# First token pair by plain products, begun among the attention tiles; the weights' further parts made later

## The chip, the cores and the metric

The kernel runs on one core of one Trainium2 chip. The metric is the time of one execution on the device in microseconds (us), the median over several runs. The engines are named as in the profile: PE is TensorE (matmuls and transposes; PEld its weight loads), DVE is VectorE, ACT is ScalarE, POOL is GpSimd and SP is SyncE, whose queue issues all DMAs of this kernel.

## The reference

Three stages follow one another. The first is chunked attention with four batches, eight heads, 768 positions and a head size of 64: each chunk of 32 queries sees 8 memory positions and a window of 56 neighbours. Its result, put together over the heads, is `x` with 3072 tokens of 512 features. The other two are feed-forward layers:

```
h = x @ w_in                        # 512 -> 2048
x = (h * tanh(softplus(h))) @ w_out # 2048 -> 512
xn = x / sqrt(mean(x*x) + 1e-6) * rms_g
g, val = xn @ w_gate, xn @ w_val    # 512 -> 1536 each
out = (silu(g) * val) @ w_out2      # 1536 -> 512
```

The weights come in 64-bit floating point, everything else in 32 bits.

## The kernel before

**Numbers.** The kernel brings each 64-bit weight tile to 32 bits itself (`cv_all`): a raw tile of 128 x 512 takes two activations on ACT (L168, L171) and three operations on DVE (L173, L174, L180). Every factor of a dense product is then split into a high and a low part (`split`: a cast on ACT, L138, and a subtraction on DVE, L139), and a product is three matmuls: high with high, high with low, low with high (`product`, L525 to L527).

**Fewer products.** A product of two 2 x 2 block matrices is done in seven block products instead of eight (`group`, in the order `ORDER`). It needs sums of blocks on both sides. On the weights' side, `cv_all` makes them after converting both tiles of a pair, and a *slot* holds seven split parts (`W_AT` gives each product's place). On the tokens' side `sum_pieces` (called through `t_pieces`) makes seven split tiles `T` for two token blocks of 384. On the way out, `group` adds up the seven results on ACT, DVE and POOL.

**Tokens and stages.** 3072 tokens are eight blocks, four pairs. Attention runs in tiles of 128 tokens, six to a pair, each in five steps a to e, which `att_list` interleaves over neighbouring tiles. The first six tiles run alone, with the first conversions between their pieces (`CV_START`). Then pair 0 goes through the first dense layer, eight groups (`group1`) with eight weight slots, while the tiles of pair 1 and the other conversions are spread over its 56 steps: `slots` returns the function `between`, which is called after every product, and which also issues stores of slots (`keep_w`), and at the end the sums and splits of the next pair (`tail_of`). Pairs 1 and 2 go alike, without conversions, but with slots reloaded (five buffers for eight slots); pair 3 has no attention beside it. Results go to memory as `g_d` through four buffers `g`.

**Afterwards** comes the second product of the first layer with the norm (`out1`, `rms_pieces`; L608 to L610), then the gated layer (`group2`), then the last product (`group3`, with `h_pieces` for sums and splits; L721 to L723).

**Order.** The tile framework orders each engine's instructions by a planner's times, and waits are put in from the data. `pin` holds an instruction behind all that was written before it for the same engine. SP issues DMAs in its own order too.

Of the kernel before, what the change touches and what calls it, by code (L numbers as in the profile page):

```python
# [24 lines left out]
W_AT = {1: 0, 2: 1, 4: 2, 3: 3, 5: 4, 6: 5, 7: 6}  # L25


@with_exitstack
def tile_kernel(
# [15 lines left out]
    nc = tc.nc  # L45
# [36 lines left out]
    cp = ctx.enter_context(tc.tile_pool(name="cp", bufs=6))  # L82
    psp = ctx.enter_context(tc.tile_pool(name="psp", bufs=1, space=bass.MemoryType.PSUM))
# [57 lines left out]
    jobs, raws, n_load = [], [], [0]  # L141
# [16 lines left out]
    def cv_all():  # L158

        done = 0  # L160
        for kind, key, parts, u, keep, store in jobs:
            tiles, slot = [], None
            for n in range(len(parts)):
                cv_prefetch(done)
                raw = raws.pop(0)
                a = cap.tile([128, 512], I32, tag="ca", name="ca")
                lr = cvp.tile([128, 512], I32, tag="lr", name="lr")
# [3 lines left out]
                nc.scalar.activation(lr, raw[:, :, 0].bitcast(U32), ACTF.Copy, scale=2.0 ** -29)  # L171
                yield
                nc.vector.tensor_scalar(a, a, 3, None, op0=ALU.logical_shift_left)  # L173
# [6 lines left out]
                nc.vector.tensor_tensor(a, a, lr, op=ALU.add)  # L180
# [11 lines left out]
            if kind == "rows":  # L192
                continue
# [10 lines left out]
            def part(i, src):  # L204
                cnt = src.shape[-1] // 256
                src = src.rearrange("p (a f) -> p a f", f=256)
                split(src, w[:, i:i + cnt, 0, :], w[:, i:i + cnt, 1, :])
# [6 lines left out]
            nc.vector.tensor_tensor(s2, s1, a11, op=ALU.subtract)  # L214
# [11 lines left out]
            yield  # L226

# [257 lines left out]
    def sum_pieces(j, b11, b21, b12, b22, new, dram, tab):  # L485
# [11 lines left out]
        def sums():  # L497
# [5 lines left out]
            nc.gpsimd.tensor_tensor(temp[4], temp[2], b21, op=ALU.subtract)  # L503
            nc.gpsimd.tensor_tensor(b12, b22, b12, op=ALU.subtract)
# [13 lines left out]
    def product(p, w, t, bank_, first):  # L518
        ws = w[:, W_AT[p]].rearrange("p l (k f) -> p l k f", k=2)
# [41 lines left out]

    def run(parts, between):
# [17 lines left out]
    def group1_parts(j, i):  # L580
# [3 lines left out]
        mul = lambda p, bank_, first: product(p, wtab["i", i], ts[p], bank_, first)  # L584
# [7 lines left out]
    def group2(j, f):  # L592
# [4 lines left out]
        mul = lambda p, bank_, first: product(p, wtab["gv", f], ts[p], bank_, first)  # L597
# [59 lines left out]
    def rms_pieces(m, n, new):  # L657
# [3 lines left out]
        sq = [cp.tile([128, N], F32, tag="c", name="sq") for _ in range(2)]  # L661
# [79 lines left out]
    CV_START = 22  # L741
# [3 lines left out]
    for i, u in zip(range(F1 // 2), W_SLOT):  # L745
        add_pair(("i", i), w_in, 2 * i, w_in, 2 * i + 1, u, True, False)
# [15 lines left out]

    first = att_list(0)
    for n, piece in enumerate(first):
# [64 lines left out]
    bt = slots((att_list(2), 56), (0, 0), tail_of(2),  # L829
               {n: keep_w(i, half) for i, ns in ((7, (1, 4)), (6, (8, 11)), (5, (15, 18)))  # L830
# [184 lines left out]
```

## Time and profile before

| | |
|---|---|
| median of 3 runs | 1231.05 us (1230.18 to 1231.24) |
| the profiled execution | 1233.01 us, its span 1231.2 us |
| granted clock of PE, mean | 0.976 of full speed |
| busy in the span | PE 95%, DVE 69%, ACT 50%, POOL 25% |
| DMA | 287.48 MB, mean 233 GB/s |

The span runs from the first to the last instruction of the program; the profiled execution's own time has 1.8 us more. All stretches below are in microseconds from the span's start. Busy time of PE counts each matmul from its start to its modelled end, and consecutive ones overlap.

### The profile page before, as it was taken

How to read it: one execution, taken by the hardware profiler on the slowest of the kernel's cores; microseconds unless marked ns; L12 is line 12 of the kernel's file. 1: busy time of each engine (PE TensorE's matmuls, PEld its weight loads, DVE VectorE, ACT ScalarE, POOL GpSimd, SP SyncE). 2: the span in 40 equal slices, each digit the busy share in tenths (PEclk: the TensorE clock that was granted, in tenths of full speed). 3: DMA queues.
4: the chain of work that ended last, by engine and by line, in shares of the span. 5: the costliest groups of instructions: out<-in, count | busy, mean ns of one | idle time of the engine just before them, and what ended most of it. 6: DMA issues, size and time to landing. Idle time of an engine off the chain costs nothing.

```text
span 1231.2 us, 24871 instructions
## 1 busy us (share of the span) xinstructions
PE 1171.6 (95%) x9896; PEld 1126.5 (91%) x9896; DVE 847.3 (69%) x1314; ACT 620.2 (50%) x1050; POOL 311.8 (25%) x251
## 2 busy tenths in 40 slices
PE   6689889999999999999999899999999999999998
PEld 4468869889999999999999899999999999999998
DVE  4598874374486876867676487766667655998883
ACT  3565543243354876677856454444444433444442
POOL 2032230030143321312111222111122121544441
PEclk8689999899999999999999999999999999999999
DMA  9689869879367874757559589969476759745540
GB/s 185 156 232 263 229 195 309 235 201 266 124 259 287 286 251 143 288 170 281 188 171 390 236 296 388 363 247 356 166 285 259 286 205 339 200 140 143 146 138 35
DMA packets 214003, 287.48 MB, mean 233 GB/s; under 512 B 103552, under 2 KB 177280, under 8 KB 209664
## 3 DMA queue, kind: packets, MB, share of 16 engines
q1 hardware_dynamic: 213888, 285.91, 70.4%
q8 instruction: 77, 1.26, 0.4%
q14 instruction: 38, 0.31, 0.1%
HBM read 180.49 MB, written 105.38 MB: 232 GB/s over the span
## 4 chain that ended last, share of the span: by engine, by line
PE 62%; DMA 8%; DVE 7%; ACT 4%; issue 2%; POOL 2%; SPq 0%; DVEq 0%; ACTq 0%; POOLq 0%
PE bk L525 10%; PE bk L526 9%; PE bk L527 9%; PE bk L721 4%; PE bk L722 4%; PE bk L723 4%; DMA T<-nt_scratch 4%; PE bk L609 2%; PE bk L610 2%; PE bk L608 2%; DMA g<-g_scratch 2%; DVE T L139 2%; PE bkp L610 1%; PE bkp L609 1%; PE bkp L608 1%
## 5 line engine op out<-in xcount | busy, mean ns | idle before, releaser
L525 PE MATMUL bk<-T,w 128*128 128x384 f32 x976 | 339.9, 350 | 13.3 <-DMA T<-nt_scratch 3.9
L526 PE MATMUL bk<-T,w 128*128 128x384 f32 x976 | 331.6, 340 | 1.9 <-DVE T L139 1.9
L527 PE MATMUL bk<-T,w 128*128 128x384 f32 x976 | 328.8, 339 | 1.7 <-DVE w L139 1.6
L525 PEld LDWEIGHTS bk<-T,w 128*128 128x128 f32 x976 | 185.8, 191 | 23.9 <-DMA T<-nt_scratch 5.3
L526 PEld LDWEIGHTS bk<-T,w 128*128 128x128 f32 x976 | 185.8, 190 | 3.5 <-DVE T L139 2.9
L527 PEld LDWEIGHTS bk<-T,w 128*128 128x128 f32 x976 | 185.3, 190 | 2.5 <-DVE w L139 2.5
L608 PE MATMUL bk<-T,w 128*128 128x384 f32 x384 | 128.9, 339 | 1.1 <-DVE s L552 1.1
L609 PE MATMUL bk<-T,w 128*128 128x384 f32 x384 | 129.8, 338 | 0.0
L610 PE MATMUL bk<-T,w 128*128 128x384 f32 x384 | 129.0, 336 | 0.0
L721 PE MATMUL bk<-w,T 128*128 128x256 f32 x396 | 111.6, 282 | 0.0
L723 PE MATMUL bk<-w,T 128*128 128x256 f32 x396 | 111.5, 282 | 0.0
L722 PE MATMUL bk<-w,T 128*128 128x256 f32 x396 | 111.3, 281 | 0.0
L552 DVE TENSOR_TENSOR s<-bk,s 128x384 f32<-128x384 f32 (+1 forms) x92 | 49.3, 536 | 89.2 <-PE bk L527 79.7
L556 POOL TENSOR_TENSOR v<-s,z 128x384 f32<-128x384 f32 x48 | 51.1, 1066 | 186.4 <-DVE s L552 103.2
L139 DVE TENSOR_TENSOR T<-w,T 128x768 fp32r<-128x768 f32 x60 | 77.4, 1301 | 11.4 <-ACT T L138 11.4
L722 PEld LDWEIGHTS bk<-w,T 128*128 128x128 f32 x396 | 75.4, 190 | 0.0
L556 POOL TENSOR_TENSOR g<-s,z 128x384 f32<-128x384 f32 x32 | 34.4, 1075 | 161.6 <-DVE s L552 85.2
L721 PEld LDWEIGHTS bk<-w,T 128*128 128x128 f32 x396 | 75.1, 190 | 0.0
L723 PEld LDWEIGHTS bk<-w,T 128*128 128x128 f32 x396 | 75.1, 190 | 0.0
L536 ACT COPY s<-bk 128x384 f32<-128x384 f32 (+1 forms) x92 | 42.6, 463 | 63.0 <-PE bk L527 52.1
L608 PEld LDWEIGHTS bk<-T,w 128*128 128x128 f32 x384 | 72.2, 188 | 1.9 <-ACT w L138 1.4
L609 PEld LDWEIGHTS bk<-T,w 128*128 128x128 f32 x384 | 72.3, 188 | 1.1 <-DVE T L139 0.3
(152 smaller groups left out, 2509.3 us busy)
## 6 DMA issues: line engine op xcount, KB each, us to landing
T<-nt_scratch SPq DMA_DIRECT2D x49, 768.0 KB
g_scratch<-g SPq DMA_DIRECT2D x64, 384.0 KB
g<-g_scratch SPq DMA_DIRECT2D x64, 384.0 KB
h_scratch<-s SPq DMA_DIRECT2D x48, 384.0 KB
w<-h_scratch SPq DMA_DIRECT2D x24, 768.0 KB
w<-wi SPq DMA_DIRECT2D x9, 1792.0 KB
nt_scratch<-T SPq DMA_DIRECT2D x21, 768.0 KB
raw<-in_moe_w_out_dram SPq DMA_DIRECT2D x28, 512.0 KB
```

What stands on the lines that cost most here:

```text
L139: (eng or nc.vector).tensor_tensor(lo, src, hi.bitcast(F32), op=ALU.subtract)
L525: nc.tensor.matmul(ps, whi, xh, start=first and kk == 0, stop=False, **more)
L526: nc.tensor.matmul(ps, whi, xl, start=False, stop=False, **more)
L527: nc.tensor.matmul(ps, wlo, xh, start=False, stop=kk == 1, **more)
L552: nc.vector.tensor_tensor(u3, y, s1, op=ALU.add)
L556: nc.gpsimd.tensor_tensor(c22, u3, z5, op=ALU.add)
L608: nc.tensor.matmul(ps, ahi, bhi, start=start, stop=False)
L609: nc.tensor.matmul(ps, ahi, blo, start=False, stop=False)
L610: nc.tensor.matmul(ps, alo, bhi, start=False, stop=stop)
L721: nc.tensor.matmul(ps, t[:, 0, f], w[:, 0], start=first and f == 0, stop=False, **more)
L722: nc.tensor.matmul(ps, t[:, 0, f], w[:, 1], start=False, stop=False, **more)
L723: nc.tensor.matmul(ps, t[:, 1, f], w[:, 0], start=False, stop=f == HG - 1, **more)
```

## The change

Pair 0 no longer goes through seven-product groups. A new `unit(b, i)` multiplies token block `b` with weight pair `i` by plain products, and results leave through ACT alone. The eight conversions of `w_in` fill only four parts of a slot (`add_plain`); the other three and the changed part 2 are made later by `finish` from the slot itself, so the parts have another order (`W_IN`). Three units of block 0 are made ready when its last attention tile is done; seven of their twelve products are put between attention pieces (`HEADS`), the rest follows the attention. Conversions are held in program order (`in_start`, whose switch `start` stays on to the end), and three slots instead of two are due before the dense part begins. The two sums of `sum_pieces` on POOL go to DVE, for every caller of it. The norm's `sq` tiles get two buffers of their own (`sqp`) instead of two of the six of `cp`.

```diff
+W_IN = {1: 0, 2: 1, 3: 2, 4: 3, 5: 4, 6: 5, 7: 6}
+    sqp = ctx.enter_context(tc.tile_pool(name="sqp", bufs=2))
-    def split(src, hi, lo, eng=None):
-        nc.scalar.copy(hi, src)
-        (eng or nc.vector).tensor_tensor(lo, src, hi.bitcast(F32), op=ALU.subtract)
+    def split(src, hi, lo, eng=None, keep=lambda ins: ins):
+        keep(nc.scalar.copy(hi, src))
+        keep((eng or nc.vector).tensor_tensor(lo, src, hi.bitcast(F32), op=ALU.subtract))
+    jobs, raws, n_load, start = [], [], [0], [True]
+
+    def in_start(ins):
+        return pin(ins) if start[0] else ins
...
+    def add_plain(key, arr, f0, f1, u):
+        jobs.append(("plain", key, [(arr, "col", f0), (arr, "col", f1)], u, True, False))
...
-                nc.scalar.activation(lr, raw[:, :, 0].bitcast(U32), ACTF.Copy, scale=2.0 ** -29)
+                in_start(nc.scalar.activation(
+                    lr, raw[:, :, 0].bitcast(U32), ACTF.Copy, scale=2.0 ** -29
+                ))
...
+                if kind == "plain":
+                    split(a.rearrange("p (a f) -> p a f", a=2), w[:, 2 * n:2 * n + 2, 0, :],
+                          w[:, 2 * n:2 * n + 2, 1, :], keep=in_start)
+                    if n == 1:
+                        wtab[key], wslot[key] = w, slot
+                    yield
+                    continue
...
+    def finish(key):
+        w = wtab[key]
+        aa = [cap.tile([128, 512], F32, tag="ca", name="ca") for n in range(2)]
+        for n, a in enumerate(aa):
+            hi, lo = (w[:, 2 * n:2 * n + 2, l, :].bitcast(F32) for l in range(2))
+            nc.vector.tensor_tensor(a.rearrange("p (a f) -> p a f", a=2), hi, lo, op=ALU.add)
+        a0, a1 = aa
+        a11, a12, a21, a22 = a0[:, 0:256], a0[:, 256:512], a1[:, 0:256], a1[:, 256:512]
+        sm = cvp.tile([128, 4, 256], F32, tag="sm", name="sm")
+        s4, s1, s2, s3 = (sm[:, i, :] for i in range(4))
+        nc.gpsimd.tensor_tensor(s1, a21, a22, op=ALU.add)
+        nc.gpsimd.tensor_tensor(s3, a11, a21, op=ALU.subtract)
+        nc.vector.tensor_tensor(s2, s1, a11, op=ALU.subtract)
+        nc.vector.tensor_tensor(s4, a12, s2, op=ALU.subtract)
+        yield
+        split(s4, w[:, 2, 0, :], w[:, 2, 1, :])
+        yield
+        split(sm[:, 1:4, :], w[:, 4:7, 0, :], w[:, 4:7, 1, :])
+        yield
...
-            nc.gpsimd.tensor_tensor(temp[4], temp[2], b21, op=ALU.subtract)
-            nc.gpsimd.tensor_tensor(b12, b22, b12, op=ALU.subtract)
+            nc.vector.tensor_tensor(temp[4], temp[2], b21, op=ALU.subtract)
+            nc.vector.tensor_tensor(b12, b22, b12, op=ALU.subtract)
...
+    def x_split(b, half):
+        t = t_new()
+        split(xb[b][:, 2 * half:2 * half + 2, :], t[:, 0], t[:, 1])
+        xtab[b, half] = t
+
+    def unit(b, i):
+        need(("i", i))
+        w = wtab["i", i]
+        g = gp.tile([128, 2, N], F32, tag="g", name="g")
+        for e in range(2):
+            ps = bk[(2 * n_unit[0] + e) % 4]
+            for half in range(2):
+                product(2 * e + half, w, xtab[b, half], ps, half == 0)
+                if half:
+                    nc.scalar.copy(g[:, e, :], ps[:, 0:N])
+                    if e:
+                        store_later(
+                            g_d[0, 2 * i:2 * i + 2, :, b, :].rearrange("f p n -> p f n"), g
+                        )
+                yield
+        n_unit[0] += 1
...
-        sq = [cp.tile([128, N], F32, tag="c", name="sq") for _ in range(2)]
+        sq = [sqp.tile([128, N], F32, tag="q", name="sq") for _ in range(2)]
...
-    CV_START = 22
+    CV_START = 24
-    for i, u in zip(range(F1 // 2), W_SLOT):
-        add_pair(("i", i), w_in, 2 * i, w_in, 2 * i + 1, u, True, False)
+    for i in (0, 1, 2, 3, 4, 5, 7, 6):
+        add_plain(("i", i), w_in, 2 * i, 2 * i + 1, W_SLOT[i])
...
+    NHEAD = 3
+    HEADS = (2, 3, 4, 5, 6, 7, 8)
+    heads, at_head = None, 10 ** 6
...
+        if piece[0] == (att_e, NSUB - 1):
+            for half in range(2):
+                x_split(0, half)
+            heads, at_head = [unit(0, i) for i in range(NHEAD)], n
+        elif n - at_head in HEADS:
+            if next(heads[0], "end") == "end":
+                heads.pop(0)
+                next(heads[0])
-    early, rest = t_pieces(0, xb.pop(0), xb.pop(1), t_new, None, ttab_x)
-    for fn in early + rest:
-        fn()
-        flush()
+    for half in range(2):
+        x_split(1, half)
+    for part in heads:
+        run([part], flush)
...
-    CV_I = 88
-    bt = slots((att_list(1), 56), (0, 98), tail_of(1),
-               {n: keep_w(i, half) for i, ns in ((0, (2, 6)), (1, (9, 13)), (2, (17, 22)))
-                for half, n in enumerate(ns)}, CV_I)
-    for i in up:
-        group1(0, i, bt)
+    CV_I = 64
+    units = [(1, i) for i in range(NHEAD)]
+    units += [(b, i) for i in (2, 3, 4, 5, 7, 6) if i >= NHEAD for b in range(2)]
+    at = {u: 4 * n + 4 for n, u in enumerate(units)}
+    more = {}
+    for i in range(3):
+        finish_at(more, i, at[1, i] + 1)
+        for half in range(2):
+            then(more, at[1, i] + 4 + 3 * half, keep_w(i, half))
+    finish_at(more, 7, at[1, 7] + 1)
+    bt = slots((att_list(1), 4 * len(units)), (0, 73), tail_of(1), calls(more), CV_I)
+    for b, i in units:
+        run([unit(b, i)], bt)
+    more = {}
+    for i, ns in ((7, (3, 5)), (6, (9, 12)), (5, (16, 19))):
+        for half, n in enumerate(ns):
+            then(more, n, keep_w(i, half))
+    for n, i in enumerate((6, 5, 4, 3)):
+        finish_at(more, i, 7 * n + 1)
+    bt = slots((att_list(2), 56), (0, 0), tail_of(2), calls(more))
```

The counts of conversion steps in the later stages are lowered to match (eight steps a slot instead of eleven); nothing else changes there.

## Rows read from the trace of the kernel before

**Rows 1.** The page's totals: busy us, share of the span, instructions.

```profile
PE 1171.6 (95%) x9896; PEld 1126.5 (91%) x9896; DVE 847.3 (69%) x1314; ACT 620.2 (50%) x1050; POOL 311.8 (25%) x251
```

**Rows 2.** Windows: length, busy us (instructions) by engine, granted clock, DMA share, GB/s.

```profile
0.00:74.00 74.00, 46.05 (x961) 34.10 (x962) 42.56 (x84) 35.79 (x61) 17.80 (x25) 0.75 0.82 172
74.00:171.60 97.60, 87.81 (x1196) 77.89 (x1197) 83.55 (x156) 56.05 (x106) 26.29 (x25) 0.96 0.92 255
171.60:260.00 88.40, 85.67 (x1133) 78.44 (x1132) 43.22 (x82) 32.09 (x58) 15.28 (x14) 0.96 0.78 231
260.00:343.40 83.40, 82.79 (x1194) 75.86 (x1194) 45.91 (x85) 33.76 (x60) 14.68 (x11) 1.00 0.63 191
...
1047.00:1231.00 184.00, 179.77 (x1505) 179.56 (x1503) 144.83 (x157) 76.49 (x119) 74.16 (x36) 1.00 0.47 134
```

**Rows 3.** Timeline of PE: start, duration, instruction; two at full, two at half clock.

```profile
98.45 0.33 PE L527 MATMUL bk<-T,w 128*128 128x384 f32 x1
98.62 0.33 PE L525 MATMUL bk<-T,w 128*128 128x384 f32 x1
...
74.64 0.52 PE L525 MATMUL bk<-T,w 128*128 128x384 f32 x1
74.96 0.52 PE L526 MATMUL bk<-T,w 128*128 128x384 f32 x1
```

**Rows 4.** The chain that ended last, two pieces of attention in pair 1.

```profile
188.61 0.79 PE bkp L423 x53
...
190.66 0.44 PE bk L406 x4
```

**Rows 5.** Groups of PE by line, 74 to 171.6 us: count, busy, mean ns, idle before.

```profile
L526 PE MATMUL bk<-T,w 128*128 128x384 f32 x110 | 38.6, 351 | 1.3 <-DVE T L139 1.3
```

**Rows 6.** Timeline around the end of the first six attention tiles.

```profile
64.21 0.59 ACT L456 COPY xb<-bk 128x512 f32<-128x512 f32 x1
...
70.72 2.25 POOL L503 TENSOR_TENSOR t<-t,xb 128x768 f32<-128x768 f32 x1
...
73.70 0.95 DVE L139 TENSOR_TENSOR T<-xb,T 128x768 fp32r<-128x768 f32 x1
...
73.84 0.69 PE L526 MATMUL bk<-T,w 128*128 128x384 f32 x1 [1.30 <-DVE T L139]
```

**Rows 7.** Waits of PE, 74 to 171.6 us: total, times, longest.

```profile
PE bk L525 <- DVE u L540: 2.6, 1, 2.6
PE bk L525 <- ACT w L138: 2.3, 3, 1.3
```

**Rows 8.** Waits of ACT, 0 to 74 us, then 74 to 171.6 us.

```profile
ACT lr L171 <- DMA raw<-in_moe_w_in_dram: 6.3, 3, 2.8
...
ACT lr L171 <- DMA raw<-in_moe_w_in_dram: 11.6, 4, 4.3
```

**Rows 9.** Groups of DVE by line and shape, 74 to 171.6 us.

```profile
L139 DVE TENSOR_TENSOR w<-sm,w 128x512 fp32r<-128x512 f32 x12 | 10.3, 875 | 3.9 <-ACT w L138 3.9
...
L139 DVE TENSOR_TENSOR T<-xb,T 128x768 fp32r<-128x768 f32 x6 | 5.6, 950 | 0.0
...
L540 DVE TENSOR_TENSOR u<-bk,s 128x384 f32<-128x384 f32 x8 | 4.4, 550 | 0.0
...
L139 DVE TENSOR_TENSOR w<-ca,w 128x512 fp32r<-128x512 f32 x5 | 3.4, 688 | 0.7 <-ACT w L138 0.7
```

**Rows 10.** The chain that ended last, near the end of pair 1.

```profile
229.60 8.60 DMA g_scratch<-g
```

**Rows 11.** Timeline of ACT and PE at the first gated groups after the norm.

```profile
696.72 0.48 ACT L544 COPY z<-bkp 128x384 f32<-128x384 f32 x1 [4.51 <-DVE w L687]
...
697.25 0.44 PE L525 MATMUL bkp<-T,w 128*128 128x384 f32 x1 [2.94 <-ACT z L544]
```

**Rows 12.** Groups of DVE and POOL by line in the last stage, 1047 to 1231 us.

```profile
L139 DVE TENSOR_TENSOR T<-w,T 128x768 fp32r<-128x768 f32 x59 | 76.5, 1307 | 11.4 <-ACT T L138 11.4
...
L503 POOL TENSOR_TENSOR t<-t,w 128x768 f32<-128x768 f32 x12 | 30.8, 2569 | 0.0
```

More of the change, by code (lines that the diff above doesn't have):

```diff
@@ L166, in cv_all @@
                 a = cap.tile([128, 512], I32, tag="ca", name="ca")
+                if kind == "plain" and n == 0:
+                    slot = w_slot(u)
+                    w = as7(slot)
                 lr = cvp.tile([128, 512], I32, tag="lr", name="lr")
@@ L179, in cv_all @@
                 yield
-                nc.vector.tensor_tensor(a, a, lr, op=ALU.add)
+                in_start(nc.vector.tensor_tensor(a, a, lr, op=ALU.add))
                 yield
                 a = a.bitcast(F32)
+                if kind == "plain":
[5 more added lines that the diff above has]
+                    continue
                 if kind == "pair":
@@ L191, in cv_all @@
                 yield
-            if kind == "rows":
+            if kind != "pair":
                 continue
@@ L206, in part @@
                 src = src.rearrange("p (a f) -> p a f", f=256)
-                split(src, w[:, i:i + cnt, 0, :], w[:, i:i + cnt, 1, :])
+                split(src, w[:, i:i + cnt, 0, :], w[:, i:i + cnt, 1, :], keep=in_start)
             if parts[0][1] == "row":
@@ L213, in cv_all @@
             yield
-            nc.vector.tensor_tensor(s2, s1, a11, op=ALU.subtract)
+            in_start(nc.vector.tensor_tensor(s2, s1, a11, op=ALU.subtract))
             nc.vector.tensor_tensor(s4, a12, s2, op=ALU.subtract)
@@ L515, in t_load, with product @@
             tab[j, p] = t
-    def product(p, w, t, bank_, first):
-        ws = w[:, W_AT[p]].rearrange("p l (k f) -> p l k f", k=2)
+    def product(at, w, t, bank_, first):
+        ws = w[:, at].rearrange("p l (k f) -> p l k f", k=2)
         ps = bank_[:, 0:N]
@@ L560, in group @@
         yield
+    def x_split(b, half):
+        t = t_new()
+        split(xb[b][:, 2 * half:2 * half + 2, :], t[:, 0], t[:, 1])
+        xtab[b, half] = t
+    xtab, n_unit = {}, [0]
+    def unit(b, i):
[14 more added lines that the diff above has]
+        n_unit[0] += 1
     def run(parts, between):
@@ L583, in group1_parts @@
         ts = {p: ttab_x[j, p] for p in ORDER}
-        mul = lambda p, bank_, first: product(p, wtab["i", i], ts[p], bank_, first)
+        mul = lambda p, bank_, first: product(W_IN[p], wtab["i", i], ts[p], bank_, first)
         banks = group_banks(4)
@@ L596, in group2 @@
         ts = {p: ttab_n[j, p] for p in ORDER}
-        mul = lambda p, bank_, first: product(p, wtab["gv", f], ts[p], bank_, first)
+        mul = lambda p, bank_, first: product(W_AT[p], wtab["gv", f], ts[p], bank_, first)
         banks = group_banks(8)
@@ L821, in reload, with then, finish_at, calls @@
             w_load(("i", seq[5 + pos]), W_SLOT[seq[5 + pos]])
-    CV_I = 88
-    bt = slots((att_list(1), 56), (0, 98), tail_of(1),
-               {n: keep_w(i, half) for i, ns in ((0, (2, 6)), (1, (9, 13)), (2, (17, 22)))
-                for half, n in enumerate(ns)}, CV_I)
-    for i in up:
-        group1(0, i, bt)
-    bt = slots((att_list(2), 56), (0, 0), tail_of(2),
-               {n: keep_w(i, half) for i, ns in ((7, (1, 4)), (6, (8, 11)), (5, (15, 18)))
-                for half, n in enumerate(ns)})
+    CV_I = 64
+    def then(more, n, fn):
+        more.setdefault(n, []).append(fn)
+    def finish_at(more, i, n):
+        part = finish(("i", i))
+        for step in range(3):
+            then(more, n + step, lambda: next(part))
+    def calls(more):
+        return {n: (lambda fns=fns: [fn() for fn in fns]) for n, fns in more.items()}
+    units = [(1, i) for i in range(NHEAD)]
[17 more added lines that the diff above has]
+    bt = slots((att_list(2), 56), (0, 0), tail_of(2), calls(more))
     for pos, i in enumerate(down):
@@ L842, in tile_kernel @@
     )
-    bt = slots(([], 56), (0, 152))
+    bt = slots(([], 56), (0, CV_I + 64))
     for pos, i in enumerate(down[:-1]):
@@ L887, in tile_kernel @@
                     pend.pop(0)()
-        cv_upto(152 + 66 * (s + 1) // len(steps))
+        cv_upto(CV_I + 64 + 66 * (s + 1) // len(steps))
         if m == NB - 1 and i in (1, 2, 4, 5):
@@ L929, in between2 @@
         return fn
-    bt = between2(284, 140)
+    bt = between2(CV_I + 196, 140)
     for jn, j in enumerate(jorder):
@@ L959, in preparing @@
         return fn
-    bt = between2(218 + 66 + 66, 125)
+    bt = between2(CV_I + 262, 125)
     for jn, j in enumerate(jback):
```

3 lines of the change are left out of this document (1 added, 2 removed).

## The prediction

> **What bounds the kernel now.** I read the page's totals first. TensorE counts as busy for 95% of the span [rows 1], which invites the conclusion that nothing is left but fewer matmuls. The windows correct that [rows 2]. In the stretch from 74 to 171.6 us, the eight groups of token pair 0, VectorE is busy 83.55 of 97.60 us and the DMA share is 0.92; in the same eight groups of pair 2, from 260 to 343.4 us, VectorE is busy 45.91 us and the DMA share is 0.63. Pair 2 takes 83.4 us, pair 0 97.6 us, and before pair 0 stand 74 us in which TensorE does hardly anything but attention.
>
> What TensorE really needs comes from starts, not durations. In back-to-back rows of the product loop a matmul starts 0.17 us after the one before (98.45, 98.62), although each lasts 0.33; where the granted clock is at half, 1.2 GHz, the step is 0.32 [rows 3]. I use 0.173. A group is 42 matmuls, 7.27 us, eight groups 58.1 us. An attention tile has two steps of 64 small matmuls at 0.79 us and four of transposes at 0.44 [rows 4], 3.34 us, six tiles 20.0 us. So a pair with attention needs 78.1 us; pair 2 loses 5.3 us beside that and pair 1 (88.4 us) 10.3. Of pair 0, 110 matmuls of the middle one of the three product lines [rows 5], so some 328 of 336 in all, lie in its stretch (the first few ran before it): 56.7 + 20.0 = 76.7 us, so it loses 20.9. From 343.4 us on TensorE has next to nothing to win back but one place at 697 us (below).
>
> The Trainium skill ("Trainium Kernel Development and Optimization", the paragraph "Reading a trace") calls matmul busy time a bad metric because matmuls are pipelined. The trace agrees: 0.33 us long, 0.17 us apart. By durations the 48 extra matmuls of this change would cost 15.8 us, by starts 8.3; the sum below uses starts.
>
> Who makes pair 0 lose its time? Ahead of it, the last rows of attention are copied out at 64.80 us, but dense products run only from 73.84: in between stand the sums on VectorE and GpSimd (one GpSimd sum alone 2.25 us) and the splits that wait for them [rows 6]. Inside it, TensorE's waits name conversions and VectorE, the longest single one 2.6 us for a drain at the changeover to pair 1 [rows 7]. ScalarE in turn waits 11.6 us for raw weights from memory [rows 8].
>
> **Part by part.** *Plain products.* A unit (one block of 384 tokens, one weight pair) is 2 x 2 x 6 = 24 matmuls, 4.15 us. Sixteen make 384, against 336: +48, 8.3 us. But 42 of them (seven products) are issued among the last pieces of the first attention tiles, so 342 remain, 59.2 us, against 56.7 in the old stretch: +2.5 us.
>
> *The start.* The unit needs no sums: after 64.80 only one ScalarE cast and one VectorE split (0.95, as in [rows 6]) stand before block 1's products, and 30 matmuls of block 0 need not even those. The dense stream could start at about 66.6. Against that, seven products lie in the in-order TensorE queue among the attention pieces: 7.3 us at full clock, 13.4 at half, where the clock here is 0.75 on average [rows 2]. The queue there mostly waits for other engines, so most of it fits; I let a quarter of 13.4 show, 3.4, and take 70.0 instead of 73.8: -4. Bounds: -7 (all hidden) and +6 (none hidden: 66.6 + 13.4 = 80).
>
> *Conversions.* By the end of that stage six raw tiles must be converted instead of four, 2 x 0.52 MB more. At the 172 GB/s of this stretch [rows 2] that is 6.1 us of transfer if none fits beside the rest; the DMA share is 0.82, so I take 0 beyond the 3.4 and keep 6.1 for the range. The switch that holds conversions in order is never turned off, so the later conversions of `w_gate`, `w_val` and `w_out2` are held as well. They are spread well ahead of their use over stages in which ScalarE and VectorE have room (pair 2: 45.91 of 83.4 us on VectorE), so 0; without that room a drain would stand behind each.
>
> *VectorE in pair 0.* Removed: 32 drains at 0.55, 17.6 us, and the splits of sums, 10.3 us. Added: four later finishes, each two rebuilding adds (bounded by the 0.69 split of the same width) and two splits of at most 0.95, 3.3 us each, 13.2 us; two sums of the tail that leave GpSimd, 1.9 us [rows 9]. The differences s2 and s4 only move. Net -12.8: some 71 us instead of 83.55, 78% of a 91 us stretch instead of 86%. ScalarE gets two copies a unit (26 for the whole units, against three a group, 24): nothing. GpSimd's adds c22 go, its s1 and s3 move.
>
> *Loss in pair 0.* With less on VectorE, no drains on the path but a copy, and ten raw tiles to load instead of twelve, the loss lies between pair 2's 5.3 us and today's 20.9. I take 12, -9. It can't go to the bottom: the stretch moves 255 GB/s x 97.6 us = 24.9 MB, 1.05 less after the change, and the same loads and stores run at 255 GB/s (231 in pair 1) [rows 2], so 23.9 MB want 94 us, part of which may overlap pair 1. The start at 70 plus 59.2 + 20.0 + 12 gives an end at 161, where it was 171.6: -10.5 in all (-4 + 2.5 - 9). Bounds -18 and +5.
>
> *Later finishes.* Slots 6, 5, 4 and 3 are finished within pair 1: 13 us more on a VectorE that is busy 43.2 of 88.4 us there [rows 2]. Nothing, as long as each comes before its group; with that cover gone 3.3 us each. The stores of slots 0 to 2 stay three and are issued some slots later; slot 5 is converted into slot 0's buffer ten steps behind the second half's store. If that store is late, the conversion waits in ScalarE's queue and behind it the copies that free TensorE's banks.
>
> *Stall in pair 1.* At 229.6 us the chain waits 8.6 us for a store of results to free its buffer [rows 10]. The number of these stores does not change, their rows on the memory side become half as long. I leave it: 0, bounds -8.6 and +4 (half of it again).
>
> *Norm's own buffers.* At 697.25 TensorE has waited 2.94 us for a copy that itself waited for VectorE's last use of a norm buffer [rows 11]. With buffers of its own the copy goes earlier, but the drain queued behind the same norm work on VectorE stays. I take -2.5, bounds 0 and -2.9.
>
> *Sums on VectorE.* In the last stage (1047 us on) VectorE takes 144.83 of 184 us, TensorE waits for nobody. Twelve tiles times two sums at 0.95 are 22.8 us more: 168 at most, still under 184. And its splits last 1.31 us there instead of 0.95, beside GpSimd sums of 2.57 [rows 9, 12], so part comes back: 0.
>
> **Sum.** -10.5 - 2.5 = -13. The profiled execution took 1233.0 us, 1.8 of it around the span of 1231.2, so the sum gives 1220 for it; it lies 2.0 us above the median of the runs, 1231.05, and so I forecast 1218.
>
> **Rivals.** *Better (0.13):* the new order of stores also dissolves the stall at 229.6. For it: it is a matter of SyncE's queue, which changes. Against: just as many bytes. 1218 - 8.6 = 1209.
>
> *Pair 0 still paced by transfers and conversion (0.16):* the start comes earlier, the loss stays at 20.9. For it: DMA share 0.92, the raw waits. Then -4 + 2.5 - 2.5 = -4, 1227.
>
> *Slower (0.15):* the conversions held in order block ScalarE. The activations wait for raw tiles, with the attention's copies queued behind them. Before, ScalarE waited 4.3 us at the longest [rows 8]; six raw tiles at 4.3 are 25.8 us, against 6.3 in three such waits of the first stage, +19.5: 1237. It decides against the change from 13 us of new waiting, some three such waits, in front of something that TensorE needs. Against it: one of the two activations was held in order already, and the first stage has slack in DMA.
>
> **Chances.** Forecast 0.56 (own range 1212 to 1224), better 0.13, transfer-paced 0.16, slower 0.15. A measurement of this kernel tells about 0.2% (2.5 us) from no change. The forecast, the better case and just over half of the transfer-paced one are faster by more: 0.78. The other part is within it: 0.07. Slower 0.15. The range leaves out most of the slower case and the far end of the better one: 1207 to 1232.
>
> **What would show it.** Right: dense products from about 70 us; pair 0's last product at about 161; VectorE near 70 us busy in that stretch; no 2.9 us gap at the first group after the last norm; all stages from 260 us on as long as before. Wrong: six ScalarE waits for raw tiles with transposes behind them; conversions still named by TensorE's waits at the end of pair 0; a new wait for finished parts in pair 1, or for the store of slot 0.

## The result and the profile after

The changed kernel takes 1207.42 us (median of 5 runs, 1205.7 to 1209.99) against 1230.18 before: the ratio is 0.9831, interval 0.981 to 0.9853. It is faster by 1.7%, 22.8 us. The forecast was 1218 us, a gain of 13: right in sign and 10.6 us too long. The measured time lies 0.4 us inside the lower end of the whole range (1207 to 1232) and outside the 1212 to 1224 that the forecast gave as its own. The profiled execution took 1208.05 us, its span 1206.3.

The first reading is where the time went. I count the product matmuls in the trace (336 for a pair in groups, 384 for pair 0 in units) and take the start of the first one behind each stage. The table has all profiled executions but two, whose times lie 6 and 11 us under their kernels' medians (they are named where they come up). Pair 0 is its end on the span, the others are lengths in us.

| kernel | median, us | pair 0 ends | pair 1 | pair 2 | pair 3 | `out1` | gated | last |
|---|---|---|---|---|---|---|---|---|
| before | 1230.2 | 171.6 | 89.1 | 82.6 | 63.3 | 277.1 | 358.5 | 189.0 |
| after | 1207.4 | 156.5 | 89.4 | 83.1 | 61.5 | 275.6 | 351.5 | 188.7 |
| e1 not held | 1224.6 | 164.8 | 92.5 | 82.0 | 64.6 | 275.4 | 353.7 | 188.7 |
| e3 before + norm | 1227.7 | 171.1 | 89.3 | 81.8 | 62.7 | 277.9 | 355.6 | 188.7 |
| e4 before + sums | 1218.9 | 163.2 | 86.1 | 82.3 | 62.6 | 273.4 | 359.6 | 188.7 |
| e5 before + norm, sums, hold | 1210.6 | 165.6 | 84.3 | 82.3 | 61.6 | 275.2 | 350.7 | 188.7 |
| e6 sums on GpSimd | 1217.1 | 158.6 | 91.4 | 82.5 | 62.9 | 282.3 | 348.8 | 188.7 |
| e7 empty finish | 1206.0 | 152.6 | 87.1 | 82.6 | 62.0 | 276.5 | 351.2 | 188.7 |
| e8 three raw buffers | 1217.3 | 163.2 | 89.3 | 82.3 | 62.3 | 275.7 | 357.0 | 188.7 |
| e9 before + norm, sums | 1212.8 | 163.3 | 88.0 | 81.4 | 63.3 | 273.2 | 353.0 | 188.7 |
| e10 hold first part | 1212.8 | 157.6 | 88.2 | 83.1 | 64.2 | 277.9 | 353.7 | 188.7 |
| e11 weights' sums on VectorE | 1206.8 | 158.0 | 89.8 | 83.5 | 62.3 | 274.5 | 352.2 | 188.1 |

So 15.1 us of the profile's 25 come from the end of pair 0, 7.0 from the gated stage, 3.3 from pair 3 and `out1`. Totals of single executions scatter by a few us, and so a stage difference under some 3 us is read only where several rows agree.

The page's totals after, busy us by engine, answer to [rows 1]:

```profile
PE 1164.7 (97%) x9944; PEld 1128.4 (94%) x9944; DVE 820.8 (68%) x1331; ACT 623.3 (52%) x1055; POOL 210.5 (17%) x203
```

TensorE has 48 instructions more, and its busy time still went down by 7 us, with a mean granted clock of 0.986 instead of 0.976. VectorE took over work from GpSimd, and its busy time went down as well, by 26.5 us. That was not in the forecast, and it is the trail to follow.

The windows of the changed kernel (length, then busy us by engine in the order PE, PEld, DVE, ACT, POOL, granted clock, DMA share, GB/s) answer to [rows 2]. The first two meet at 62.7 us, behind the transposes of the last of the first six attention tiles, where the dense products run on:

```profile
0.00:62.70 62.70, 45.61 (x936) 37.03 (x937) 33.64 (x74) 33.51 (x58) 7.55 (x17) 0.84 0.94 192
62.70:156.50 93.80, 84.57 (x1246) 77.52 (x1244) 66.16 (x122) 53.17 (x101) 16.14 (x17) 0.97 0.91 252
...
156.50:246.00 89.50, 87.54 (x1196) 79.80 (x1194) 59.04 (x112) 41.08 (x75) 15.67 (x17) 0.97 0.84 255
246.00:329.00 83.00, 81.57 (x1156) 74.99 (x1157) 43.77 (x86) 32.30 (x58) 8.57 (x8) 1.00 0.63 187
...
1017.60:1206.30 188.70, 184.56 (x1537) 184.36 (x1535) 142.22 (x185) 79.40 (x122) 16.41 (x13) 1.00 0.49 141
```

VectorE is busy 66.16 of 93.80 us in pair 0, 71%, where the forecast had 71 us and 78%. DMA is as full as before, 0.91. Clock and DMA share of the first stage rose, from 0.75 and 0.82 [rows 2] to 0.84 and 0.94.

In the timeline of TensorE the units now run inside that first stage, from 46 us on at full clock; the spacing is again 0.17 us:

```profile
44.51 1.31 PE L566 MATMUL bk<-T,w 128*128 128x384 f32 x3
...
46.03 0.34 PE L566 MATMUL bk<-T,w 128*128 128x384 f32 x1
46.21 0.33 PE L567 MATMUL bk<-T,w 128*128 128x384 f32 x1
...
60.78 0.60 PE L490 MATMUL bk<-ident,x 128*128 128x128 f32 x4
```

The last of the first six attention tiles is transposed at 60.78 us. Its copy, in ScalarE's timeline, begins 2.6 us earlier than before (64.21 [rows 6]), although products now stand in between:

```profile
61.60 0.59 ACT L497 COPY xb<-bk 128x512 f32<-128x512 f32 x1
```

One line's count behind that point, from the groups of TensorE between 62.7 and 156.5 us, answers to [rows 5]:

```profile
L567 PE MATMUL bk<-T,w 128*128 128x384 f32 x108 | 37.0, 342 | 0.0
```

That is 3 x 108 = 324 of 384: sixty were done by 62.7 us. 324 x 0.173 + 20.0 = 76.1 us of need, in 93.8 us: pair 0 still loses 17.7 us, against 20.9 before.

The waits in that part, TensorE's from 40 us on and ScalarE's from 60, answer to [rows 7] and [rows 8]:

```profile
PE bkp L415 <- DVE kw L360: 3.8, 1, 3.8
PE bk L490 <- ACT qT L405: 2.3, 2, 1.7
...
ACT ca L180 <- DMA raw<-in_moe_w_in_dram: 15.5, 6, 5.7
```

TensorE's waits for conversions are all but gone; what it waits for is attention. The longest is at the changeover. There the chain that ended last runs over VectorE:

```profile
150.27 0.95 DVE xb L542
...
153.20 0.87 DVE t L543
154.07 1.41 DVE xb L545
155.47 0.18 DVE kw L360
...
155.70 0.89 PE bkp L415 x38
```

L542 to L545 are the sums for pair 1, now all on VectorE. A small copy that an attention tile needs (L360) stands behind three of them in VectorE's queue, and TensorE stands 3.8 us; a product behind it lasts as long as those at half clock in [rows 3], in TensorE's timeline:

```profile
157.00 0.52 PE L567 MATMUL bk<-T,w 128*128 128x384 f32 x1
```

The move of the sums to VectorE is not what makes this gap: with two of them back on GpSimd (e6 below) TensorE waits at the same place, in e6's waits from 135 to 170 us:

```profile
PE bkp L415 <- DVE kw L360: 2.8, 1, 2.8
```

The wait is missing in e1, e7, e11 and e12; which of the works at the changeover makes it was not tried alone.

### The profile page after: what moved, and what is told of

Read it like the earlier page. It is cut to its first block, busy times and chain, and to the rows that moved or that the text cites. A ratio compares the mean times of both kernels' runs of the same rounds, so it can differ in the third digit from the quotient of the medians.

```text
span 1206.3 us, 24873 instructions
## 1 busy us (share of the span) xinstructions
PE 1164.7 (97%) x9944; PEld 1128.4 (94%) x9944; DVE 820.8 (68%) x1331; ACT 623.3 (52%) x1055; POOL 210.5 (17%) x203
## 4 chain that ended last, share of the span: by engine, by line
PE 81%; DMA 7%; DVE 6%; ACT 3%; issue 2%; SPq 1%; POOL 0%; DVEq 0%; ACTq 0%; POOLq 0%
PE bk L566 13%; PE bk L567 12%; PE bk L568 12%; PE bk L674 4%; PE bk L673 4%; PE bk L675 4%; PE bk L786 4%; PE bk L787 4%; PE bk L788 4%; DMA raw<-in_moe_w_in_dram 2%; PE bkp L566 2%; PE bkp L568 2%; PE bkp L567 2%; PE bkp L675 2%; PE bkp L674 2%; PE bkp L673 2%
## 5 line engine op out<-in xcount | busy, mean ns | idle before, releaser
L566 PEld LDWEIGHTS bk<-T,w 128*128 128x128 f32 x992 | 187.3, 189 | 10.6 <-DMA T<-nt_scratch 2.8
L593 DVE TENSOR_TENSOR s<-bk,s 128x384 f32<-128x384 f32 (+1 forms) x84 | 45.0, 536 | 91.2 <-PE bk L568 81.7
L141 DVE TENSOR_TENSOR T<-g,T 128x768 fp32r<-128x768 f32 x64 | 66.0, 1048 | 20.9 <-ACT T L140 20.8
L141 DVE TENSOR_TENSOR T<-w,T 128x768 fp32r<-128x768 f32 x60 | 58.8, 991 | 23.9 <-ACT T L140 23.1
L140 ACT CAST T<-w 128x768 fp32r<-128x768 f32 x60 | 49.3, 833 | 47.5 <-PE bk L788 28.4
```

The source lines that it names most:

```text
L140: keep(nc.scalar.copy(hi, src))
L141: keep((eng or nc.vector).tensor_tensor(lo, src, hi.bitcast(F32), op=ALU.subtract))
L566: nc.tensor.matmul(ps, whi, xh, start=first and kk == 0, stop=False, **more)
```

## Experiments

Each ratio is against the kernel before, run on the same chip.

**e1: conversions not held in order.**

```diff
-    jobs, raws, n_load, start = [], [], [0], [True]
+    jobs, raws, n_load, start = [], [], [0], [False]
```

> The changed kernel with the hold on program order off (one activation of each raw tile stays held, as before). Theory 'order': the hold lets the first attention stage end 3.4 us earlier (61.4 against 64.8 us) although more raw tiles pass through it, and keeps the conversions of pair 0 from standing in front of attention; without it the first product of block 1 and the end of pair 0 come 3 to 8 us later, 1211 to 1215 us. Rival 'units': the early end comes from plain units alone, which need no sums, and the hold does nothing: 1207 us, within 2. The case against the hold (my slower rival): it costs, and without it the kernel is faster, under 1205.

Measured: 1224.64 us, ratio 0.9955 (0.9933 to 0.9978). Seventeen us slower than the full change by the medians, 15 by the ratios, more than either theory gave. Without the hold the units cost time: the same kernel with groups in their place (e9 below) takes 1212.75 us. My slower rival had the sign wrong. The timeline of ScalarE, e1, shows why:

```profile
41.51 0.62 ACT L140 CAST w<-ca 128x512 fp32r<-128x512 f32 x1 [1.47 <-DVE ca L194]
47.98 0.66 ACT L183 ACTIVATE lr<-raw 128x512 int32<-128x512 uint32 x1 [5.85 <-DMA raw<-in_moe_w_in_dram]
48.54 0.61 ACT L434 ACTIVATE p<-p 128x512 f32<-128x512 f32 x1
```

Not held, the second activation of a raw tile (L183) was put ahead of an attention tile's exponential (L434). The raw tile came 5.85 us late, and the exponential waited in the queue. TensorE paid for it, in e1's timeline:

```profile
49.21 1.11 PE L447 MATMUL bk<-ident,p 128*128 128x128 f32 x4 [5.12 <-ACT p L434]
```

The last of the first six attention tiles is copied out at 70.51 us in e1, where the changed kernel has 61.60.

In the changed kernel the exponential goes first, and the raw tile of that moment is waited for behind it:

```profile
42.38 0.63 ACT L434 ACTIVATE p<-p 128x512 f32<-128x512 f32 x1 [0.86 <-DVE p L429]
...
47.74 0.66 ACT L180 ACTIVATE ca<-raw 128x512 f32<-128x512 f32 x1 [1.65 <-DMA raw<-in_moe_w_in_dram]
```

**e2: no product written among the attention pieces.**

```diff
-    HEADS = (2, 3, 4, 5, 6, 7, 8)
+    HEADS = ()
```

> The changed kernel with no product written among the attention pieces (HEADS empty); the three units of block 0 are still made ready in the middle and run behind the last piece. Theory 'filling': some 70 products that ran before 62.7 us now come after it, 70 x 0.173 = 12 us, less what the planner moves ahead by itself: 1213 to 1219 us, and the granted clock of the first stage falls back to about half. Rival 'planner': the planner moves the ready matmuls ahead anyway, and the time stays at 1207 us within 2.

Measured: 1214.05 us, ratio 0.9849 (0.9814 to 0.9884). The time lies in the range of the theory 'filling', and the interval overlaps the full change's. The profiled execution (1203.13 us) is far off the median, so its stages decide nothing about the time; but it shows the order of the instructions. The first product runs at 44.0 us, as in the full change (44.5), and by 62.7 us as many are done, 3 x 20, at the same mean granted clock of 0.84, in e2's windows and groups:

```profile
0.00:62.70 62.70, 45.59 (x933) 37.20 (x934) 34.02 (x74) 33.02 (x57) 7.64 (x17) 0.84 0.96 192
...
L567 PE MATMUL bk<-T,w 128*128 128x384 f32 x20 | 7.2, 360 | 0.0
```

The planner moves ready matmuls into the gaps by itself, so the mechanism of 'filling' is not there. Why the median is 6.6 us above the full change's, and whether that is the written places, stays open.

**e3: the kernel before with the norm's own buffers alone.**

```diff
+    sqp = ctx.enter_context(tc.tile_pool(name="sqp", bufs=2))
-        sq = [cp.tile([128, N], F32, tag="c", name="sq") for _ in range(2)]
+        sq = [sqp.tile([128, N], F32, tag="q", name="sq") for _ in range(2)]
```

> The kernel before, with the norm's own two buffers alone. Theory of the forecast: the gap of 2.9 us at 697 us goes, nothing else: 2.5 us less than before. Rival, from the trace after: the gated stage is 7.0 us shorter (351.5 us instead of 358.5), and most of it is this edit: 5 to 7 us less. If neither, the gain of that stage is the sums' move to VectorE: 0.

Measured: 1227.7 us, ratio 0.9969 (0.9951 to 0.9987), 3.3 us; the gated stage is 2.9 us shorter. TensorE's waits of that stage in e3:

```profile
PE bk L526 <- DMA T<-nt_scratch: 5.3, 4, 3.1
PE bkp L526 <- ACT z L545: 0.6, 1, 0.6
```

The copy's 2.94 us [rows 11] have become 0.6. This term was as forecast.

**e4: the kernel before with the two sums of `sum_pieces` on VectorE alone.**

```diff
-            nc.gpsimd.tensor_tensor(temp[4], temp[2], b21, op=ALU.subtract)
-            nc.gpsimd.tensor_tensor(b12, b22, b12, op=ALU.subtract)
+            nc.vector.tensor_tensor(temp[4], temp[2], b21, op=ALU.subtract)
+            nc.vector.tensor_tensor(b12, b22, b12, op=ALU.subtract)
```

> The kernel before, with the two sums of sum_pieces on VectorE alone. Theory of the forecast: 0 within 1.5 us, since TensorE covers it, but the start of pair 0 needs these sums and may come 1 to 3 us earlier (a GpSimd sum takes 2.25 us, a VectorE one 0.95). Rival: the sums' move frees the token tiles' splits from contention in all stages and gives 3 to 7 us, most of it in the gated stage, whose waits for tiles from memory follow the stores of these splits.

Measured: 1218.87 us, ratio 0.9904 (0.9877 to 0.9932): 12 us from two changed words, more than either expectation. By stages 8.4 us lie in pair 0, 3.0 in pair 1, 3.7 in `out1`. The rival named the gated stage, which did not move. At the start of pair 0, where dense products run from 70.10 us instead of 73.84 (3.7 of the 8.4 us), VectorE in the kernel before, while GpSimd sums (L504 and L503, [rows 6]):

```profile
69.21 2.09 DVE L139 TENSOR_TENSOR w<-ca,w 128x512 fp32r<-128x512 f32 x1
71.22 2.56 DVE L139 TENSOR_TENSOR T<-t,T 128x768 fp32r<-128x768 f32 x1
73.70 0.95 DVE L139 TENSOR_TENSOR T<-xb,T 128x768 fp32r<-128x768 f32 x1
```

and the same place in e4:

```profile
67.77 0.94 DVE L503 TENSOR_TENSOR t<-t,xb 128x768 f32<-128x768 f32 x1
68.63 0.68 DVE L139 TENSOR_TENSOR w<-ca,w 128x512 fp32r<-128x512 f32 x1
69.24 0.94 DVE L139 TENSOR_TENSOR T<-t,T 128x768 fp32r<-128x768 f32 x1
```

The sum itself takes 0.94 us instead of 2.25, and two subtractions beside it 0.68 and 0.94 instead of 2.09 and 2.56.

**e5: the kernel before with norm's buffers, sums on VectorE and conversions held, its groups kept.** The edits of e3 and e4, and `pin` around the same five conversion steps as in the change:

```diff
-                nc.vector.tensor_tensor(a, a, lr, op=ALU.add)
+                pin(nc.vector.tensor_tensor(a, a, lr, op=ALU.add))
```

> The kernel before with its seven-product groups in pair 0 and no units, but with the three other parts of the change: norm's own buffers, the two sums on VectorE, conversions held in order. Theory 'hold': in the earlier runs sums alone gave 12 us and norm alone 3, and the full change without the hold lost 17 us of its gain; so it is these three and not the plain products that shorten the time: 1207 us within 4. Rival 'units': the hold only pays because the units need no sums and fill the first stage; with groups the held conversions come late: 1214 to 1222 us, and the first product stays near 48 us with the end of pair 0 at 160 us or later.

Measured: 1210.56 us, ratio 0.984 (0.9804 to 0.9875). The interval covers the full change (0.9831): beside the other three parts, the plain products, the largest part of the diff, bring no gain that can be measured (3 us by the medians, 1 by the ratios, with some 5 us of room to either side). They do end pair 0 nine us earlier (156.5 against 165.6). Pair 1 then gives five back (89.4 against 84.3). Its window in e5, 165.6 to 249.9 us, against the third one of the changed kernel above:

```profile
165.60:249.90 84.30, 83.52 (x1114) 75.99 (x1112) 43.08 (x84) 31.66 (x57) 12.70 (x12) 1.00 0.82 247
```

VectorE has 16 us less to do there, and the clock stays at 1.00: no gap like the 3.8 us of the changed kernel stands right ahead of it (TensorE's longest wait from 156 us on is 0.8).

**e6: the changed kernel with the sums back on GpSimd** (the edit of e4, reversed).

> The changed kernel with the two sums of sum_pieces back on GpSimd. Theory, from the run with the sums alone (12 us): most of the gain lay at the start of pair 0, which units don't need, so undoing costs less here, 3 to 7 us: 1210 to 1214 us. Rival: the two edits add, 1219 us. If 1207 within 2, the units have made the sums' move worthless.

Measured: 1217.11 us, ratio 0.9902 (0.9868 to 0.9935): 9.7 us lost. Most of it is not at the start, which units have freed of these sums, but 4 us by the end of pair 1 and 6.7 in `out1`, of which the gated stage returns 2.7. So the sums' move is worth nearly as much with units as without, and in other places. The splits of the token tiles in e6, groups of VectorE up to 345 us:

```profile
L141 DVE TENSOR_TENSOR T<-xb,T 128x768 fp32r<-128x768 f32 x19 | 23.5, 1259 | 0.7 <-ACT T L140 0.5
...
L141 DVE TENSOR_TENSOR T<-t,T 128x768 fp32r<-128x768 f32 x6 | 7.5, 1252 | 1.6 <-ACT T L140 1.6
```

and in the changed kernel:

```profile
L141 DVE TENSOR_TENSOR T<-xb,T 128x768 fp32r<-128x768 f32 x19 | 18.9, 1012 | 0.7 <-ACT T L140 0.6
L141 DVE TENSOR_TENSOR T<-t,T 128x768 fp32r<-128x768 f32 x6 | 5.7, 947 | 0.0
```

**e7: finish without arithmetic.** The further parts of a slot are filled with zeros by GpSimd, so the first layer's products of pairs 1 to 3 are others.

```diff
-        aa = [cap.tile([128, 512], F32, tag="ca", name="ca") for n in range(2)]
...
-        nc.vector.tensor_tensor(s4, a12, s2, op=ALU.subtract)
+        nc.gpsimd.memset(w[:, 2, :, :].bitcast(F32), 0.0)
         yield
-        split(s4, w[:, 2, 0, :], w[:, 2, 1, :])
+        nc.gpsimd.memset(w[:, 4:7, :, :].bitcast(F32), 0.0)
         yield
-        split(sm[:, 1:4, :], w[:, 4:7, 0, :], w[:, 4:7, 1, :])
         yield
```

(left out here: the other adds and sums of `finish`)

> The changed kernel in which finish does no arithmetic: the slot's parts 2 and 4 to 6 are filled with zeros by GpSimd instead of being made, so the first layer's result for pairs 1 to 3 is another. Some 4 us of VectorE and 1.3 of ScalarE fall away for each of eight slots. Theory 'VectorE' for the 19 us that pair 0 still loses: its end comes 5 to 10 us earlier than 156.5, 1198 to 1203 us. Rival 'raw tiles': what it waits for are raw weights from memory, held in order; then the end moves by less than 3 us, 1205 to 1208.

Measured: 1206.01 us, ratio 0.9802 (0.9766 to 0.9838), not told apart from the full change. In the profile, which is 3.5 us under the median, pair 0 ends 3.9 us earlier. VectorE is busy 53 us between 61 and 156 us there, against 66 in the full change; taking 13 us off it does not take the loss away. Even the 3.9 us are not sure to come from it: the executions of e2 and e12, in which VectorE has its full load, end pair 0 at 153.5 and 152.3 us.

**e8: three raw buffers, loaded three ahead** (and, for room, norm's own buffers given back).

```diff
-    rawp = ctx.enter_context(tc.tile_pool(name="rawp", bufs=2))
+    rawp = ctx.enter_context(tc.tile_pool(name="rawp", bufs=3))
-        while n_load[0] < len(flat) and n_load[0] - done < 2:
+        while n_load[0] < len(flat) and n_load[0] - done < 3:
```

> The changed kernel with three buffers for raw tiles instead of two, loaded three ahead; to make room, the norm's own buffers are given back (about 3 us in the gated stage). Theory 'raw tiles': ScalarE's 15.5 us of waits for raw tiles in pair 0 shrink to under 5 and pair 0 ends 4 to 10 us before 156.5. Rival 'VectorE' or 'transfers': it ends within 2 us of 156.5, because the queue and the DMA engines carry no more, and the total is 1210 us.

Measured: 1217.29 us, ratio 0.9899 (0.986 to 0.9938), slower than the full change by 10 us. ScalarE's waits for raw tiles fell as meant, from 15.5 us to this (60 to 163 us):

```profile
ACT ca L179 <- DMA raw<-in_moe_w_in_dram: 3.9, 2, 3.5
```

and pair 0 still ended at 163.2 us, 6.7 later; the last of the first six attention tiles is copied out 3.3 us later (64.89). TensorE now waits for attention's own loads, in e8 from 40 to 163 us:

```profile
PE bk L350 <- DMA kn<-in_k_dram: 2.2, 1, 2.2
PE bkp L463 <- DMA vw<-in_v_dram: 1.7, 2, 1.0
```

Raw tiles loaded earlier go ahead of keys and values on the same queue: SyncE issues the third one at 13.1 us, in the changed kernel at 26.7. That late raw tiles cost pair 0 its time is not borne out: making them earlier moves the wait. The gated stage is 5.5 us longer; the norm's buffers, given back, were worth 2.9 of that in e3.

**e9: the kernel before with norm's buffers and sums, conversions not held** (the edits of e3 and e4 together).

> The kernel before with norm's own buffers and the sums on VectorE, conversions not held. Theory 'parts add': 3 + 12 = 15 us less than before, 1215 us; then holding conversions is worth 4 to 5 us beside groups (1210.6 with it), against 17 us beside units (1224.6 without it, 1207.4 with it). Rival: norm and sums overlap, 1219 us, and the hold is worth 8 or more beside groups too.

Measured: 1212.75 us, ratio 0.9862 (0.9835 to 0.9889), 17.8 us. The two small edits make up three quarters of the whole gain. With e1, e5 and the full change this makes a square, in which all four kernels have the norm's buffers and the sums on VectorE:

| median, us (ratio) | not held | held |
|---|---|---|
| groups | 1212.75 (0.9862, e9) | 1210.56 (0.984, e5) |
| units | 1224.64 (0.9955, e1) | 1207.42 (0.9831, the full change) |

Beside groups the hold adds 2 us that the intervals don't tell apart; beside units it decides over 15 to 17 us. Without the hold the units make the kernel some 12 us slower, and the intervals lie well apart; with it they are not told apart from groups. Pair 0 in e9, in windows from the start of its dense products to its end:

```profile
71.70:163.30 91.60, 86.90 (x1201) 77.30 (x1200) 82.03 (x157) 57.58 (x108) 20.34 (x23) 0.98 0.94 265
```

It is 2 us shorter than the stretch of the changed kernel (93.80 us), with VectorE busy for 90% of it.

**e10: conversions held only until pair 0 is done.**

```diff
     for n, i in enumerate((6, 5, 4, 3)):
         finish_at(more, i, 7 * n + 1)
+    start[0] = False
```

> The changed kernel with conversions held in order only up to the end of pair 0; those of w_out, w_gate, w_val and w_out2 float as before. Theory: the hold's worth lies where attention's copies and conversions share ScalarE, so the end of pair 0 stays at 156.5 us, and later stages give up the 5 us by which pair 3 and the gated stage were shorter: 1210 to 1213 us. Rival: all of the hold's 17 us come from the first 160 us and what follows from them: 1207 within 2.

Measured: 1212.83 us, ratio 0.9863 (0.9837 to 0.9889); the interval overlaps the full change's at its edge. Pair 0 ends at 157.6, as with the full hold (156.5). Pair 3, `out1` and the gated stage are 2.7, 2.3 and 2.2 us longer. So the hold's part before 160 us is the larger one, and of the rest some 5 us are likely, not settled.

**e11: the weights' sums s1 and s3 on VectorE too.**

```diff
-            nc.gpsimd.tensor_tensor(s1, a21, a22, op=ALU.add)
-            nc.gpsimd.tensor_tensor(s3, a11, a21, op=ALU.subtract)
+            nc.vector.tensor_tensor(s1, a21, a22, op=ALU.add)
+            nc.vector.tensor_tensor(s3, a11, a21, op=ALU.subtract)
```

(in `cv_all` and in `finish`)

> The changed kernel with the weights' sums s1 and s3 on VectorE too, in conversions and in finish (two operations of about 0.42 us each instead of two of 0.8 on GpSimd). Theory 'contention': what the tokens' sums won by leaving GpSimd came from VectorE operations with two inputs from SBUF no longer being lengthened beside them; then s2 (0.94 us now) falls to 0.42 and the chain of finish shortens: 2 to 5 us less, 1202 to 1205. Rival 'size': those operations were 2.3 us, these are 0.8 and run where nothing waits: 1207 within 2.

Measured: 1206.76 us, ratio 0.9805 (0.9775 to 0.9834). No difference from the full change that can be measured, so the rival 'size' has the time right. The lengthening did go, as the other theory had it. The subtraction s2 of `finish`, groups of VectorE up to 400 us, in the changed kernel and in e11:

```profile
L261 DVE TENSOR_TENSOR sm<-sm,ca 128x256 f32<-128x256 f32 x8 | 6.7, 840 | 4.6 <-POOL sm L259 4.6
...
L261 DVE TENSOR_TENSOR sm<-sm,ca 128x256 f32<-128x256 f32 x8 | 3.9, 486 | 0.0
```

It falls from 840 to 486 ns, and nothing that the total shows waited for it.

**e12: the edit of e11, and the group's addition c22 on VectorE as well.**

```diff
-        nc.gpsimd.tensor_tensor(c22, u3, z5, op=ALU.add)
+        nc.vector.tensor_tensor(c22, u3, z5, op=ALU.add)
```

> As the run before, and the group's last addition c22 on VectorE too (0.55 us instead of 1.1 on GpSimd, 72 times). Theory 'contention': again less, 1199 to 1204. Rival: VectorE's queue gets longer just where each group's drains end (four in a row instead of three), and TensorE waits for its banks: the gain is lost, 1206 to 1212.

Measured: 1205.91 us, ratio 0.9798 (0.9769 to 0.9828). Again none; the rival's time, though its mechanism is not shown, since the profiled execution (1199.55 us) is 6 us off the median. No version here is clearly faster than the changed kernel.

## Why the prediction came out as it did

The sign was right for reasons that were on record (an earlier start, the norm's buffers). That the time lies in the range, by 0.4 us, is luck. The forecast put 10.5 of its 13 us on the plain products, and e5 gains 18.6 us without them; two parts that it booked at nothing, the sums' move and the hold, carry most of the gain. Of its signs, the early dense products, the end of pair 0 and VectorE's load were met or passed, and the norm's gap went; that all stages from 260 us on stay as long did not come (the gated one is 7.0 us shorter), and one sign of being wrong did, six waits of ScalarE for raw tiles (15.5 us).

*The start: -4 forecast, bounds -7 and +6; measured -11.* The dense stream runs from 62.7 us instead of 73.84. Not a quarter of the inserted products showed, but nothing: attention ended 2.6 us earlier in spite of them. The step that failed was to cost the hold on order at nothing and to count only its risk. e1 shows it: without the hold a conversion stands ahead of an exponential, TensorE waits 5.1 us, the first attention tiles end 8.9 us later (70.51 us), and pair 0 ends at 164.8.

*Products: +2.5 forecast; measured -0.7.* Sixty matmuls ran early, not 42, so 324 stayed instead of 342. The planner places them by itself (e2).

*Loss in pair 0: -9 forecast; measured -3.2.* VectorE's load fell somewhat more than worked out, to 66 us, and the loss stayed at 17.7. e7 takes VectorE's work away and e8 ScalarE's waits for raw tiles, and neither brings pair 0 to pair 2's 5.3 us; e9 loses less, 14.5 us (91.6 less a need of 77.1, for 330 of its 336 matmuls), with VectorE busy for 82 us. So the load on VectorE, from which the term was worked out, is not what sets it. TensorE's own waits between 62.7 and 156.5 us come to 9.1 us: 3.8 at the changeover, 0.8 for a conversion, the others for attention. Pair 2's 5.3 and, as an estimate from the mean granted clock of 0.97, 2 to 3 us of lower clock make up the rest. The forecast's own bound, 23.9 MB at 255 GB/s in 94 us, fits the length, but 255 is no ceiling: e9 moves 265 GB/s in this part. That transfers set the waits was not tried alone (fewer bytes, the rest unchanged), and so it stays open. The three terms together gave -10.5, measured -15.1: the start came out 7 us better than forecast, the products 3 better and the loss 6 worse, and a sum hides such errors.

*Later finishes in pair 1: 0 forecast; measured 0 against the kernel before, +5 against e5.* It looks like nothing because the sums' move had made pair 1 shorter by 3 us at the same time (e4). How much of the 5 us is the finishes is not separated: e7, without them, is 2.3 us shorter, but it also lacks the half clock that the changed kernel has for the first 5.3 us of pair 1 behind the gap (its mean over pair 1 is 0.97, in e7 1.00). The execution of e12 has the finishes and a clock of 1.00, and its pair 1 takes 84.9 us, which speaks for the clock and against the finishes.

*Stall in pair 1: 0 forecast.* The chain of the changed kernel waits 2.40 us for a store where it had 8.60 [rows 10]:

```profile
219.69 2.40 DMA g_scratch<-g
```

Pair 1 is no shorter for it, so the rival "better" named a place that is not where the time came from.

*Norm's buffers: -2.5 forecast; measured -2.9 in the stage, -3.3 in all (e3).* Right.

*Later conversions held: 0 forecast.* e10 lets them float again and is 5 us slower by the medians, 2.2 of it in the gated stage, though the intervals overlap. With the norm's 2.9 that makes 5.1 of the gated stage's 7.0 us; the rest is not placed.

*Sums on VectorE: 0 forecast; measured -12 alone (e4), -9.7 as their share in the change (e6).* This is the term that was mis-sized most. I worked it out where it changes nothing, in the last stage, and there it was right: that stage is 188.7 us with and without. VectorE's load there, from its groups in the changed kernel, answers to [rows 12]:

```profile
L141 DVE TENSOR_TENSOR T<-w,T 128x768 fp32r<-128x768 f32 x59 | 57.9, 992 | 23.9 <-ACT T L140 23.1
...
L544 DVE TENSOR_TENSOR t<-t,w 128x768 f32<-128x768 f32 x12 | 11.4, 950 | 0.0
```

The split fell from 1307 ns to 992 and the moved sum takes 950 ns where GpSimd took 2569. The same stretching held at the changeovers between pairs and in `out1`, here in VectorE's timeline of the kernel before:

```profile
637.48 2.60 DVE L139 TENSOR_TENSOR T<-T 128x768 fp32r<-128x768 f32 x1
```

There time was won when the sums moved (e4, e6), and for those places I had booked only 1.9 us of added load. A row of the stretch in question, 2.25 us of GpSimd beside a split that waits, was in front of me [rows 6]; I used it for the old start and not for the other callers of the same function.

*Rivals.* Transfer-paced: its loss of 20.9 us was nearer to the measured 17.7 than mine of 12, while its time, 1227, was off because of the start and the sums. Better: its 1209 was the nearest number of all, by another way than its own. Slower: refuted with the opposite sign by e1.

## What to carry to other kernels

Where an edit moves work from one engine to another, list every caller of the function and look in each stage for what waits on it; the stage with the highest load need not be the one that pays. Operations of two engines side by side are priced by rows in which both run and by rows in which one runs alone. Hold back, in program order, what waits for memory on an engine that also serves a latency chain: here the planner put such an activation first, and the exponential behind it waited out its 5.85 us (e1). And try the parts of a change apart and in pairs: here two small edits made three quarters of the gain, and the largest one cost time without the hold.

## What the hardware showed that was not expected

VectorE gained free time by taking on more work: 847.3 us busy before, 820.8 after, while GpSimd fell from 311.8 to 210.5. The Trainium skill ("SBUF — State Buffer", section "Who interferes with whom") says that a VectorE instruction with two inputs from SBUF contends with a GpSimd instruction that reads SBUF, and one with at most one such input, outside its two-port modes, does not. The traces agree on both: the 768-column split, two inputs from SBUF, takes 0.94 us alone (e4) and up to 2.56 beside a GpSimd sum (the kernel before), and the drain, which takes one of its inputs from PSUM, has the same mean as before, in the profile's groups of the changed kernel:

```profile
L593 DVE TENSOR_TENSOR s<-bk,s 128x384 f32<-128x384 f32 (+1 forms) x84 | 45.0, 536 | 91.2 <-PE bk L568 81.7
```

536 ns in both kernels. The mean hides no lengthened ones: counted by their overlap in the trace of the kernel before, additions and subtractions of 384 columns with one input from PSUM take 0.55 us where they run at least half of their time beside such an operation on GpSimd, and 0.55 us where they run beside none. Nor is every operation with two inputs from SBUF longer beside GpSimd: the sum L502 on VectorE, begun just ahead of L504 on GpSimd, keeps 0.96 us in the last stage. By that rule of the Trainium skill e11 relieves VectorE as well (840 to 486 ns above); that it shows no gain says that a contention costs time only where something waits for it.
